# Five moments of issue in a hand-ordered attention and feed-forward kernel on one core

## The chip, the cores and the metric

The kernel runs on one core of one Trainium2 chip. The metric is the device time of one execution in microseconds (us). The engines are called TensorE (PE in the rows; PEld is its loading of weights, which overlaps the matmuls), VectorE (DVE), ScalarE (ACT), GpSimd (POOL) and SyncE (SP), which here only issues DMAs. Each engine works through its own instructions in the order in which the program gives them, and waits on semaphores for the others. Lnnn is a line of the kernel before.

## The reference

Queries, keys and values have 4 batches, 8 heads, 1152 positions and 64 channels. Two neighbouring queries are averaged, so that 576 remain; attention follows. Its output, 4 x 576 x 512, goes through a block that mixes positions and channels by the real part of a two-dimensional Fourier transform, a normalization, and a feed-forward of 512 to 2048 to 512 with two residual sums:

```python
q_pool = q.reshape(B, H, S // 2, 2, D).mean(axis=3)
scores = scale * q_pool @ k.transpose(0, 1, 3, 2)
x = softmax(scores) @ v                      # then (B, 576, 512)
u = x + real(fft(fft(x, axis=1), axis=2))
un = (u - mean(u)) / sqrt(var(u) + 1e-6)
out = u + relu(un @ w_ch1) @ w_ch2
```

The inputs are fp32, with the feed-forward weights handed over as raw 64-bit words that the kernel itself turns into numbers.

## The kernel before

**Attention.** The 32 heads go in 16 pairs, each pair in 5 units (units 0 to 3 take 128 queries of each of the two heads, unit 4 the last 64 of both). For a unit TensorE makes the scores in three pieces of 384 keys (s_piece, L209; two matmuls each, one with the rounded queries qh and one with the rest ql), DVE moves them out with a running bound, ACT takes the exponent in place (s_exp), TensorE transposes the result (t_step, L247), ACT or DVE copies the transposed tiles to SBUF (L250), and TensorE multiplies them with the values (av, L263); ACT copies that into the x buffer of the batch (L267). While unit n is transposed, the scores of unit n+1 are made. The product of a unit (finish, L410) is issued in the next unit, behind its first two score pieces.

**A head's preparation.** In unit 0 and unit 2 of a pair load_head issues the loads of the next pair's two heads: k by POOL's queue, queries, half of k and v by SyncE's queue. There is one buffer qr of raw queries. In units 1 and 3 prep_head (L180) has POOL add neighbouring queries (L186) and make the low part of k (L189); a later event, q_high (L192), has ACT round the queries to qh (L194) and POOL make the rest ql (L197).

**Feed-forward.** Four batches are transformed (dft), normalized (norm) and fed forward (ffn) one after the other. ffn of a batch has 32 blocks in the order q, which, i: four blocks f1 (512 tokens through 128 of the 2048 channels, 12 matmuls, L685 to L687, then ACT's relu L704 and DVE's low part L705) and four blocks f2 (12 matmuls, DVE adds to x at L717). The last four f2 blocks, 28 to 31, end the batch's output and issue its stores (L719). Each block's weights, 512 KB, are read from a scratch in DRAM two blocks ahead into one of three buffers (L677). The last batch also takes the 64 tokens of each batch that the others leave out, works with 384 tokens in two halves, and runs alone at the end.

**Raw weights.** 32 conversions (convert, L614) make that scratch while attention runs: SyncE loads 512 KB of raw words (L617) into one of three buffers, and steps of ACT (L626, L632, L643), DVE (L628, L630, L636, L639) and POOL (L646) follow; SyncE stores the result (L652). From L621 to L649 one conversion is inside at a time; others ask again every 400 units (L619). At most three are under way. A block of the first batch is not issued before the conversion of the block two further on has issued its store (L740). The tiles named wa, rest and wb are taken in turn from four buffers.

**The order.** Nothing is scheduled by a compiler. The program keeps a planner's clock, now, in units of about a nanosecond. attention() yields after each piece of TensorE work and names its cost; each cost gives credit (0.98 or 0.85 of it) to background(), which issues steps of mids (dft and norm, each with a due time) and fills (ffn; 2720 units a block) as long as there is credit. after(wait, fn) puts a step into a heap; it is issued at the first yield whose now is late enough. So a number in after or in a yield decides where in the order of every engine a step stands, and nothing else. When attention is over (tail), fills are issued while mids are not yet due.

**den_recip** (L269) has DVE take the reciprocals of a pair's sums; an event later TensorE transposes them (L276), ACT copies them, SyncE writes them to DRAM and spreads them over 128 rows, and POOL multiplies x by them (DVE in every fourth pair, after which dft of that batch is begun).

**drain** (L793) issues mids and fills, with conversions and events, until block 2h+1 of the last four of a batch has been issued. There are five x buffers (XB); from the sixth on a new one takes the place of one whose output must have been stored, and finish() calls drain just before the first product that is written to it (L411 to L413).

**dft** of the last batch has no gaps between its steps (gap is 0), but two waits of 1200 (L444) and 1800 units (L487): the first behind copies of single rows, the second behind the folds that DVE makes (L450 to L476), ahead of the first transform on TensorE (L497).

Of the kernel before, what the change touches and what calls it, by code (L numbers as in the profile page):

```python
# [12 lines left out]
F32 = mybir.dt.float32  # L13
F32R = mybir.dt.float32r
I32 = mybir.dt.int32
U32 = mybir.dt.uint32
AF = mybir.ActivationFunctionType
# [7 lines left out]
P = 128  # L25
# [18 lines left out]
NP = B * H // 2  # L44
# [10 lines left out]
def fused_kernel(ctx: ExitStack, tc: tile.TileContext, k2, q2, v2, w1, w2, cst, out):  # L55
    nc = tc.nc
# [3 lines left out]
    XB = 5  # L60
# [6 lines left out]
    cvp = pool("cv", 1)  # L67
# [112 lines left out]
    def prep_head(n):  # L180
        kr, qr, ks, vs = raw.pop(n)
        qh, ql = alloc_q(n)
        o = q_cols(n)[0]
        pieces = ((0, SQ, 0),) if o == 512 else ((0, 512, 0), (512, SQ, o))
        for c in (slice(0, HT), slice(HT, SQ)):
            nc.gpsimd.tensor_tensor(qr[:, 0, c], qr[:, 0, c], qr[:, 1, c], op=ALU.add)  # L186
        for i in range(4):
            c = slice(i * HT, i * HT + HT)
            nc.gpsimd.tensor_tensor(ks[D:, c], kr[D:, c], ks[D:, c].bitcast(F32), op=ALU.subtract)  # L189
        qkv[n] = ks, qh, ql, vs  # L190

        def q_high():  # L192
            for a, b, c in pieces:
                nc.scalar.copy(qh[:, c:c + b - a], qr[:, 0, a:b])  # L194
                for x, y in ((a, a + HT), (a + HT, b)) if b - a > HT else ((a, b),):
                    z = slice(c + x - a, c + y - a)
                    nc.gpsimd.tensor_tensor(ql[:, z], qr[:, 0, x:y], qh[:, z].bitcast(F32), op=ALU.subtract)  # L197
        after(2600, q_high)

    sp = {}  # L200
    den = {}
# [54 lines left out]
    def av(pr, j, where):  # L256

        po = ps_o.tile([P, P], F32, tag="o", name="o")
        w = P if j < 4 else D
        for c in range(NKC):  # L260
            for y in range(2):
                pt, o = where[y, c]
                nc.tensor.matmul(po[y * D:y * D + D, :w], lhsT=qkv[2 * pr + y][3][:, c, :], rhs=pt[:, o:o + w],  # L263
                                 start=c == 0, stop=c == NKC - 1)
        if pr not in xt:
            xt[pr] = xt[pr + 1] = xp.tile([P, 2, SQ], F32, tag="x", name="x")
        nc.scalar.copy(xt[pr][:, pr % 2, j * P:j * P + w], po[:, :w])  # L267
# [40 lines left out]
    def attention():  # L308
        first = [load_first(0), load_first(1)]
        for n, (q_load, _, k_load, _, _) in enumerate(first):  # L310
            k_load(*K0[0])
            q_load(*Q0[0])
            for c in K0[1:]:
                k_load(*c)
        nc.sync.dma_start(ident, cst[4, :, :P])
        for q_load, _, _, _, v_load in first:
            q_load(*Q0[1])
        for q_load, _, _, _, v_load in first:
            v_load()
            q_load(*Q0[2])  # L320
        units = [(pr, j) for pr in range(NP) for j in range(5)]
        def parts(n):
            _, q_part, _, k_part, _ = first[n]
            k_part(*K0[0])
            yield q_part(*Q0[0])
            yield k_part(*K0[1])
            yield k_part(*K0[2])

        for _ in parts(0):
            pass  # L330
        for pc, _ in enumerate(parts(1)):
            s_piece(0, 0, pc)
        for _, q_part, _, _, _ in first:
            q_part(*Q0[1])
        s_exp(0, 0)
        for pc in range(3):
            s_piece(1, 0, pc)
        s_exp(1, 0)
        nc.sync.dma_start(onesm, cst[4, :, P:2 * P])
        for _, q_part, _, _, _ in first:  # L340
            q_part(*Q0[2])
        yield 2000
        held = None
        for i, (pr, j) in enumerate(units):
            if pr == 1 and j == 0:
                for x, (t, r) in enumerate(((cc1, P), (cs1, P), (cc2, 97), (cs2, 97))):
                    n, m = t.shape[1:]
                    for r0, r1 in ((0, r // 32 * 32), (r // 32 * 32, r)):
                        if r0 < r1:
                            nc.sync.dma_start(t[r0:r1], cst[x, r0:r1, :n * m].rearrange("p (a b) -> p a b", a=n))  # L350
            if pr + 1 < NP:
                if j in (0, 2):
                    load_head(2 * pr + 2 + j // 2)
                if j in (1, 3):
                    prep_head(2 * pr + 2 + j // 2)
            nxt = unit_tiles(*units[i + 1]) if i + 1 < len(units) else []
            pieces = deque((n, jj, pc) for n, jj in nxt for pc in range(3))
            expd = []

            def some(k):  # L360
                pe = 0
                for _ in range(k):
                    if pieces:
                        p = pieces.popleft()
                        pe += s_piece(*p)
                        if p[2] == 2:
                            expd.append(p[:2])
                return pe

            def exps():  # L370
                while expd:
                    s_exp(*expd.pop(0))

            tiles = unit_tiles(pr, j)
            where = {}

            def tr(items, eng):
                pt = t_step(pr, [(k, c) for k, c, _ in items], eng)
                for x, (_, _, ys) in enumerate(items):
                    for y, o in ys:  # L380
                        where[y, items[x][1]] = pt, x * P + o
                return 105 * len(items)

            if j < 4:
                a, b = tiles
                ga = [[(a, c, [(0, 0)]) for c in cs] for cs in (range(4), range(4, 8))]
                gb = [[(b, c, [(1, 0)]) for c in cs] for cs in (range(4), range(4, 8))]
                gc = [(a, 8, [(0, 0)]), (b, 8, [(1, 0)])]
                g = [ga[0], ga[1], gb[0], gb[1], gc]
            else:  # L390
                k = tiles[0]
                g = [[(k, c, [(0, 0), (1, D)]) for c in cs] for cs in (range(4), range(4, 8), range(8, 9))]
            yield some(2)
            if held:
                yield finish(*held)
            yield tr(g[0], "a")
            yield some(2)
            yield tr(g[1], "a")
            yield some(2)
            for y, x in enumerate(g[2:]):  # L400
                yield tr(x, "v" if j < 4 and y == 1 else "a")
            exps()
            if j == 4:
                after(1500, den_recip(pr))
            held = pr, j, where
            for k in tiles:
                sp.pop(k)
        yield finish(*held)

    def finish(pr, j, where):  # L410
        if j == 0 and pr % 2 == 0 and pr // 2 >= XB:  # L411

            drain(*divmod(pr // 2 - XB, 2))  # L413
        av(pr, j, where)
        if j == 4:
            for y in range(2):
                qkv.pop(2 * pr + y)
        return 1950 if j < 4 else 1000
# [4 lines left out]
    def dft(b):  # L423
# [17 lines left out]
        nc.vector.tensor_copy(ua[D:D + 1, 1, :], tmp[D:D + 1, 0, :])  # L441
        yield 0, gap
        nc.scalar.copy(ub[D:D + 1, 0, :], tmp[D:D + 1, 1, :])
        yield 0, 1200  # L444
        xs = []
        for y, op in ((1, ALU.subtract), (0, ALU.add)):

# [36 lines left out]

        yield from fold(1)
        yield from fold(0)
        yield 0, 1800  # L487

        for y, n in ((1, 256), (0, 257)):

# [121 lines left out]
    going = []  # L612

    def convert(f, which):  # L614
        src = (w1, w2)[which]
        w = cvp.tile([P, 512, 2], I32, tag="wraw", name="wraw", bufs=3)
        nc.sync.dma_start(w, src[f].bitcast(I32).rearrange("p (c x) -> p c x", x=2))  # L617
        yield 4000 if going else 7000
        while inside:  # L619
            yield 400  # L620
        inside.append(f)  # L621
# [6 lines left out]
        nc.vector.tensor_scalar(a, a, WORD_MIN, WORD_MAX, op0=ALU.max, op1=ALU.min)  # L628
        yield 700 if going else 1000
        nc.vector.tensor_scalar(ai, ai, 3, 0x3FFFFFF8, op0=ALU.logical_shift_left, op1=ALU.bitwise_and)  # L630
        rest = cvp.tile([P, 512], F32, tag="cv", name="rest", bufs=4)
        nc.scalar.activation(rest, low.bitcast(U32), AF.Copy, scale=2.0 ** -52)  # L632
        yield 700 if going else 1000
        t = cvp.tile([P, 512], F32, tag="cv", name="wb", bufs=4)
        b = t.bitcast(I32)
# [2 lines left out]
        yield 700 if going else 1000  # L638
        nc.vector.tensor_scalar(ai, b, -0x800000, None, op0=ALU.bitwise_and)  # L639
        yield 700 if going else 1000  # L640
        h = w.rearrange("p c x -> p (c x)").rearrange("p (x c) -> p x c", x=2)
        hi, lo = h[:, 0, :], h[:, 1, :]
        nc.scalar.copy(hi.bitcast(F32R), t)  # L643
# [141 lines left out]
    def after(wait, fn):  # L785

        heapq.heappush(events, (now + wait, next(tick), fn))
# [5 lines left out]
    def drain(b, h):  # L793
        nonlocal now, due, credit
        while (b, 2 * h + 1) not in done_f2:
            if mids and now >= due:
                c = step(mids)
                if c:
                    now += c[0]
                    credit -= c[0]  # L800
                    due = now + c[1]
                continue
            c = step(fills)
            now += c or 300
            credit -= c
            conversions()
            run_events()
# [116 lines left out]
```

## Time and profile before

| | us |
|---|---|
| median of 3 runs | 1041.01 |
| lowest and highest | 1038.89, 1047.71 |
| the profiled execution, its own time | 1044.25 |
| its span, first to last instruction | 1042.5 |
| mean granted share of TensorE's clock | 0.981 |

[...] A row of the waits view is: engine, tile and line that waited, what it waited for, then the sum in us, how often, and the longest. A row of the timeline is: start, duration, engine, line, operation, tiles, shape, count, and in brackets the engine's idle time before it and what ended it.

### The profile page before, as it was taken

Reading aid. Unit: us, or ns where it says so; the run is one execution under the profiler, and the core shown is the slowest. Engines: PE = TensorE matmul, PEld = TensorE weight load, DVE = VectorE, ACT = ScalarE, POOL = GpSimd, SP = SyncE. Lnnn points to the kernel's source line nnn. Section 1 sums busy time; section 2 is a strip of 40 time slices with the busy share of each in tenths; the row PEclk is TensorE's granted clock in tenths of the full one; section 3 lists DMA queues with packets and bytes.
Section 4 is the critical chain, followed back from the end, with each engine's and each line's share of the span. In section 5 each row is a group of like instructions: output and inputs, shape, how many; then the busy total and the mean of one; then the engine's idle time right before and its main releaser. Section 6 shows DMA issues by size and latency. Waiting matters only on the chain.

```text
span 1042.5 us, 19731 instructions
## 1 busy us (share of the span) xinstructions
PE 975.8 (94%) x7392; PEld 847.5 (81%) x7392; DVE 605.4 (58%) x1518; ACT 523.7 (50%) x1017; POOL 421.7 (40%) x609
## 2 busy tenths in 40 slices
PE   6999988898998899899999999999999989999998
PEld 4898977777877777687788888787788867899998
DVE  5556868889754687787644475666544245522222
ACT  5778877767745566466444554554444231201100
POOL 3555678788386575996323141633200010000000
PEclk9999999999999899999999999999999989999999
DMA  6545467646566856475745464163532334733443
GB/s 186 170 135 180 135 197 239 183 127 221 143 203 243 276 181 220 140 240 187 217 145 179 135 193 129 33 207 109 170 104 102 115 120 126 230 134 122 126 136 122
DMA packets 62515, 170.91 MB, mean 164 GB/s; under 512 B 16770, under 2 KB 20242, under 8 KB 62420
## 3 DMA queue, kind: packets, MB, share of 16 engines
q1 hardware_dynamic: 58100, 151.96, 46.1%
q0 software_dynamic: 4320, 17.70, 5.3%
q8 instruction: 58, 0.95, 0.4%
q14 instruction: 37, 0.30, 0.1%
HBM read 146.88 MB, written 22.75 MB: 163 GB/s over the span
## 4 chain that ended last, share of the span: by engine, by line
PE 50%; DVE 5%; POOL 3%; ACT 2%; DMA 2%; issue 1%; SPq 0%; DVEq 0%; ACTq 0%; POOLq 0%
PE f L685 7%; PE f L687 6%; PE f L686 6%; PE s L220 6%; PE o L263 5%; PE t L247 5%; PE t L685 4%; PE t L687 4%; PE t L686 4%; DVE sp L222 1%; DMA out<-x 1%; PE f L505 1%; DMA w<-w 1%; POOL wb L646 1%; POOL rest L646 0%
## 5 line engine op out<-in xcount | busy, mean ns | idle before, releaser
L222 DVE TENSOR_SCALAR_CACHE_REDUCE sp<-s,bia 128x384 f32<-128x384 f32 x288 | 177.2, 615 | 79.2 <-PE s L220 57.2
L220 PE MATMUL s<-ks,qh 128*128 128x384 f32 x480 | 185.7, 387 | 19.8 <-ACT qh L164 6.4
L234 ACT ACTIVATE sp<-sp,bia 128x1152 f32<-128x1152 f32 x144 | 180.2, 1256 | 1.8 <-DVE sp L222 1.6
L263 PE MATMUL o<-pt,vs 128*64 128x128 f32 (+1 forms) x2880 | 171.7, 273 | 9.4 <-DVE pt L250 5.0
L263 PEld LDWEIGHTS o<-pt,vs 128*64 128x64 f32 x2880 | 151.5, 141 | 33.6 <-issue 20.7
L250 ACT COPY pt<-t 128x512 f32<-128x512 f32 (+2 forms) x243 | 124.5, 527 | 91.3 <-PE t L247 90.2
L220 PE MATMUL s<-ks,ql 128*128 128x384 f32 x480 | 164.9, 344 | 0.4 <-POOL ql L165 0.4
L247 PE MATMUL t<-ident,sp 128*128 128x128 f32 x1045 | 150.6, 276 | 7.1 <-DVE sp L222 3.7
L247 PEld LDWEIGHTS t<-ident,sp 128*128 128x128 f32 x1045 | 121.5, 141 | 28.3 <-DVE sp L222 6.7
L220 PEld LDWEIGHTS s<-ks,qh 128*128 128x128 f32 x480 | 92.4, 193 | 31.7 <-ACT pt L250 9.0
L189 POOL TENSOR_TENSOR ks<-kr,ks 64x288 fp32r<-64x288 f32 x120 | 103.4, 894 | 29.7 <-issue 12.6
L705 DVE SCALAR_TENSOR_TENSOR g<-f,g 128x512 fp32r<-128x512 f32 (+1 forms) x52 | 34.7, 667 | 110.0 <-ACT g L704 110.0
L220 PEld LDWEIGHTS s<-ks,ql 128*128 128x128 f32 x480 | 93.1, 194 | 1.1 <-POOL ql L165 0.8
L704 ACT ACTIVATE g<-f 128x512 fp32r<-128x512 f32 (+1 forms) x52 | 30.1, 579 | 119.7 <-PE f L687 119.7
L186 POOL TENSOR_TENSOR qr<-qr 128x288 f32<-128x288 f32 x60 | 49.9, 850 | 92.6 <-DMA qr<-in_q 92.6
L197 POOL TENSOR_TENSOR ql<-qr,qh 128x288 fp32r<-128x288 f32 (+2 forms) x75 | 55.7, 768 | 75.0 <-ACT qh L194 73.7
L685 PE MATMUL f<-unh,w 128*128 128x512 f32 (+1 forms) x208 | 82.8, 398 | 2.7 <-DMA w<-w 2.7
L646 POOL TENSOR_TENSOR rest<-rest,wa 128x256 f32<-128x256 f32 x64 | 48.2, 770 | 89.2 <-DVE wa L639 64.0
L222 DVE TENSOR_SCALAR_CACHE_REDUCE sp<-s 128x384 f32<-128x384 f32 x144 | 78.4, 545 | 6.1 <-PE s L220 4.4
L687 PE MATMUL f<-unl,w 128*128 128x512 f32 (+1 forms) x208 | 80.4, 387 | 0.0
L686 PE MATMUL f<-unh,w 128*128 128x512 f32 (+1 forms) x208 | 80.2, 386 | 0.0
L685 PE MATMUL f<-g,w 128*128 128x512 f32 (+1 forms) x188 | 74.2, 394 | 1.9 <-DVE g L705 0.9
(149 smaller groups left out, 1761.3 us busy)
## 6 DMA issues: line engine op xcount, KB each, us to landing
w<-w SPq DMA_DIRECT2D x128, 512.0 KB
qr<-in_q SPq DMA_DIRECT2D x30, 576.0 KB
ks<-in_k POOLq DMA_DIRECT2D x30, 576.0 KB, 6.1
wraw<-in_w SPq DMA_DIRECT2D x32, 512.0 KB
w<-wraw SPq DMA_DIRECT2D x32, 512.0 KB
vs<-in_v SPq DMA_DIRECT2D x32, 288.0 KB
kr<-in_k SPq DMA_DIRECT2D x30, 288.0 KB
out<-x SPq DMA_DIRECT2D x12, 256.0 KB
```

The costliest lines, as they stand in the source:

```text
L189: nc.gpsimd.tensor_tensor(ks[D:, c], kr[D:, c], ks[D:, c].bitcast(F32), op=ALU.subtract)
L197: nc.gpsimd.tensor_tensor(ql[:, z], qr[:, 0, x:y], qh[:, z].bitcast(F32), op=ALU.subtract)
L220: nc.tensor.matmul(ps, lhsT=l, rhs=k, start=i == 0, stop=i == len(ops) - 1)
L222: nc.vector.tensor_scalar(sp[n, j][:, c], ps, -0.0625, bt[:, pc - 1:pc] if pc else None, op0=ALU.mult, op1=ALU.min, accum_out=bt[:, pc:pc ...
L234: last_exp[0] = nc.scalar.activation(t, t, AF.Exp, bias=bia.pop((n, j))[:, 2:3], scale=-1.0, accum_out=den[pr][:, col:col + 1]).ins
L247: nc.tensor.transpose(ps[:, i * P:i * P + P], sp[k][:, c * P:(c + 1) * P], ident)
L250: (nc.vector.tensor_copy if eng == "v" else nc.scalar.copy)(pt[:, :o], ps[:, :o])
L263: nc.tensor.matmul(po[y * D:y * D + D, :w], lhsT=qkv[2 * pr + y][3][:, c, :], rhs=pt[:, o:o + w], start=c == 0, stop=c == NKC - 1)
L646: nc.gpsimd.tensor_tensor(o[:, c], x[:, c], y[:, c], op=op)
L685: nc.tensor.matmul(ps, lhsT=ah, rhs=bh, start=first, stop=False)
L686: nc.tensor.matmul(ps, lhsT=al, rhs=bh, start=False, stop=False)
L687: nc.tensor.matmul(ps, lhsT=ah, rhs=bl, start=False, stop=last)
```

## The change

Five places are changed, none of which adds or removes an instruction:

- convert: the step behind the load comes 6500 instead of 4000 units later once ffn has begun (going), and the ACT copy rest, with its buffer, is taken three steps later, just ahead of the rounding of the high part;
- prep_head: q_high is issued 5000 instead of 2600 units later;
- den_recip: the transpose is issued 3000 instead of 1500 units later, except in every fourth pair;
- finish: drain for the next pair's x buffer is also called in unit 2 of the pair before;
- dft of the last batch: 1200 becomes 2400, and 1800 becomes 6000.

```diff
@@ prep_head
-        after(2600, q_high)
+        after(5000, q_high)
@@ attention
-                after(1500, den_recip(pr))
+                after(3000 if pr % 4 < 3 else 1500, den_recip(pr))
@@ finish
+        if j == 2 and pr % 2 and (pr + 1) // 2 >= XB and pr + 1 < NP:
+            drain(*divmod((pr + 1) // 2 - XB, 2))
         av(pr, j, where)
@@ dft
-        yield 0, 1200
+        yield 0, 1200 if gap else 2400
...
-        yield 0, 1800
+        yield 0, 1800 if gap else 6000
@@ convert
-        yield 4000 if going else 7000
+        yield 6500 if going else 7000
...
-        rest = cvp.tile([P, 512], F32, tag="cv", name="rest", bufs=4)
-        nc.scalar.activation(rest, low.bitcast(U32), AF.Copy, scale=2.0 ** -52)
         yield 700 if going else 1000
         t = cvp.tile([P, 512], F32, tag="cv", name="wb", bufs=4)
...
         nc.vector.tensor_scalar(ai, b, -0x800000, None, op0=ALU.bitwise_and)
         yield 700 if going else 1000
+        rest = cvp.tile([P, 512], F32, tag="cv", name="rest", bufs=4)
+        nc.scalar.activation(rest, low.bitcast(U32), AF.Copy, scale=2.0 ** -52)
         h = w.rearrange("p c x -> p (c x)").rearrange("p (x c) -> p x c", x=2)
```

## Rows read from the trace of the kernel before

**Rows 1.** Page, part 1: busy us of each engine, share of span, instructions.
```profile
PE 975.8 (94%) x7392; PEld 847.5 (81%) x7392; DVE 605.4 (58%) x1518; ACT 523.7 (50%) x1017; POOL 421.7 (40%) x609
```

**Rows 2.** Windows: PE, PEld, DVE, ACT, POOL busy, clock, DMA share, GB/s.
```profile
125.00:525.00 400.00, 361.22 (x2880) 303.81 (x2876) 292.06 (x697) 251.63 (x487) 279.37 (x386) 0.96 0.62 198
```

**Rows 3.** Waits of the whole span: who <- whom, sum us, times, longest us.
```profile
ACT x L267 <- DMA out<-x: 20.4, 2, 11.4
...
ACT wa L626 <- DMA wraw<-in_w: 16.4, 3, 6.5
ACT qh L194 <- POOL qr L186: 15.3, 7, 3.4
...
ACT rest L632 <- POOL rest L646: 10.6, 4, 4.0
...
DVE wb L636 <- POOL wraw L646: 8.2, 6, 2.2
...
PE t L276 <- DVE den L272: 5.9, 8, 1.5
```

**Rows 4.** Timeline of SP, ACT and PE, 347 to 364: start, us, what, [idle <-releaser].
```profile
347.66 0.34 SPq L652 DMA_DIRECT2D w<-wraw  x1
354.95 0.33 SPq L617 DMA_DIRECT2D wraw<-in_w  x1
...
358.63 0.66 ACT L626 ACTIVATE wa<-wraw 128x512 f32<-128x512 f32 x1 [6.47 <-DMA wraw<-in_w]
...
359.81 4.10 PE L263 MATMUL o<-pt,vs 128*64 128x128 f32 x34 [3.86 <-ACT pt L250]
```

**Rows 5.** Windows behind three of TensorE's waits.
```profile
358.00:365.00 7.00, 5.19 (x37) 4.66 (x38) 3.60 (x7) 5.29 (x10) 4.58 (x7) 0.51 0.89 311
846.00:853.00 7.00, 4.86 (x18) 4.37 (x19) 4.33 (x10) 2.57 (x7) 0.00 (x0) 0.52 0.10 42
299.00:303.00 4.00, 3.48 (x18) 2.98 (x19) 1.93 (x5) 2.54 (x5) 3.92 (x6) 1.00 0.86 317
```

**Rows 6.** Timeline: three waits of PE; POOL and PE at head 9.
```profile
299.52 0.44 PE L220 MATMUL s<-ks,qh 128*128 128x384 f32 x1 [1.72 <-ACT pt L250]
...
432.52 0.44 PE L220 MATMUL s<-ks,qh 128*128 128x384 f32 x1 [2.22 <-DVE sp L222]
442.09 1.19 PE L247 MATMUL t<-ident,sp 128*128 128x128 f32 x6 [2.14 <-DVE sp L222]
...
142.77 1.69 POOL L197 TENSOR_TENSOR ql<-qr,qh 128x288 fp32r<-128x288 f32 x3
144.42 1.43 POOL L646 TENSOR_TENSOR rest<-rest,wa 128x256 f32<-128x256 f32 x2
...
144.57 0.34 PE L220 MATMUL s<-ks,qh 128*128 128x384 f32 x1
```

**Rows 7.** Timeline of PE behind ACT's two waits for output stores.
```profile
507.52 0.93 PE L247 MATMUL t<-ident,sp 128*128 128x128 f32 x6 [2.50 <-ACT pt L250]
...
737.41 0.44 PE L220 MATMUL s<-ks,qh 128*128 128x384 f32 x1 [1.56 <-ACT pt L250]
```

**Rows 8.** Windows: L685 alone (PE, PEld, clock, DMA), and five blocks back to back.
```profile
461.00:499.50 38.50, 11.39 (x28) 5.26 (x28) 1.00 0.62 211
...
824.46:838.18 13.72, 13.72 (x62) 11.34 (x61) 4.12 (x6) 2.00 (x4) 0.00 (x0) 1.00 0.71 207
```

**Rows 9.** Timeline of SP: stores of conversion 29 and of the last, 31.
```profile
472.15 0.32 SPq L652 DMA_DIRECT2D w<-wraw  x1
...
491.95 0.36 SPq L652 DMA_DIRECT2D w<-wraw  x1
```

**Rows 10.** Timeline of PE and DVE in the last transform and normalization.
```profile
848.14 0.74 PE L497 MATMUL t<-cs,xs 128*97 128x128 f32 x2 [4.36 <-DVE xs L473]
...
896.84 0.18 DVE L565 RECIPROCAL vt<-vt 96x6 f32<-96x6 f32 x1
...
901.05 1.43 DVE L597 TENSOR_TENSOR unl<-d,unh 128x576 fp32r<-128x576 f32 x2
```

## Prediction

> **What bounds the kernel now.** I read the page first. TensorE's matmuls are busy for 975.8 us of a span of 1042.5 [rows 1]; no other engine passes 81%, and TensorE's weight loads, which overlap the matmuls, are the one that reaches it. The program is one long TensorE queue, so an edit is worth what it takes out of TensorE's 66.7 us of idle time, plus what the clock gives back. The windows then say where that idle time lies: between 125 and 525 us, where raw weights are converted beside attention, TensorE is busy for 361.22 of 400 us, so 38.8 us of the 66.7 are there, and the mean granted clock is 0.96 [rows 2]. [...] Third, the list of waits: the reader is to look for waits of ScalarE (ACT) and VectorE (DVE) on things that are merely late, since both engines work in order and TensorE waits for them in turn [rows 3]. The rows shown are those that an edit touches. All terms below are made against the profiled execution, 1044.25 us: its span and 1.75 us around it. That is 3.2 above the median of the runs, 1041.01.
>
> **Raw weights (L618, L631).** Nothing is added: 32 conversions keep their instructions. The step that reads the loaded weights is issued 6500 instead of 4000 planner units after the load. What happens now: SyncE may start the load only when the buffer's store has landed, here 354.95 us for a store issued at 347.66; ACT already stands at the step, idle for 6.47 us, until 358.63, and TensorE gets its transposed tile 3.86 us late [rows 4]. There are three such waits, 16.4 us of ACT [rows 3]; only this one shows on TensorE at more than 1 us. 2500 units are some 3 us here, and a conversion that would have jumped the queue with data still in flight now finds an older one ahead of it, so I count 3.9. No weight comes too late for it: conversions run one at a time between L621 and L649 and wait there anyway.
> The copy called rest moves three steps later. It stops ACT 4 times, 10.6 us, for a buffer that GpSimd (POOL) still reads, and DVE 6 times, 8.2 us, in the opposite order of allocation [rows 3]. With the tiles allocated in the new order DVE's step needs the buffer freed by POOL's first pair of operations, and the copy the one freed by its last; but the copy is issued three steps of 700 units later, which are some 3 us here, and POOL's two other pairs take 2 x 1.43 [rows 6]. The TensorE wait at 432.52 us, 2.22 us, stands behind both [rows 6]. Sum 3.9 + 2.2: I take -6, bounds -9 (two smaller waits go too) and +3 (the copy now stands right before the one that POOL waits for).
>
> **Rounded queries (L198).** The ACT copy is issued 5000 instead of 2600 units after POOL's addition that it reads. ACT waited 7 times, 15.3 us, for that addition [rows 3]; TensorE's waits at 299.52 and 442.09, 1.72 and 2.14 us, follow two of them [rows 6], and I count about as much again for the other five: -7.7. Against it: the copy is followed by POOL's subtraction (ql), and POOL is in order. For head 9 ql ended at 142.77 + 1.69 = 144.46 and TensorE read the head at 144.57; directly behind ql stood a conversion, three pairs of POOL operations of 1.43 us, the first at 144.42 [rows 6]. If these are now issued first, ql comes 4.3 us later and TensorE waits about as much. For other heads I add 1.5. SyncE's load of the next head's queries waits for ql also, for up to 2400 units more; that costs only where the next head has no room either, and stands in the upper bound. Together -2; bounds -8 and +10 (three heads caught).
>
> **Transposed reciprocals (L404).** TensorE's transpose waits 8 times for DVE's reciprocal, 5.9 us [rows 3]. In 12 of 16 pairs it is issued 1500 units later, that is behind at least one more unit of TensorE work; the longest wait is 1.5. The other four pairs keep their share. -4, bounds -5 and 0; the scaling behind it is not urgent in these pairs.
>
> **Output stores (L411).** Now the feed-forward of a batch is forced to its output stores at the moment when the next x buffer is wanted. ACT waits for these stores twice, 20.4 us [rows 3]; TensorE then waits 2.50 at 507.52 and 1.56 at 737.41 [rows 7]. Forced three units of attention earlier, the stores have landed: -4. But the forced work is larger. The first time it starts near 460 us, and from 461 to 499.5 TensorE ran 28 of the L685 matmuls, 4 to a block, so 7 blocks must now come in one piece; a block is 13.72 / 5 = 2.74 us [rows 8], together 19.2. Blocks 27 to 29 can be issued only when conversions 29 to 31 have been, of which the stores left at 472.15 and (the last) 491.95 [rows 9]. TensorE runs out of work about 479 us. The conversions then have ACT, DVE and POOL nearly to themselves, and block 29 itself needs only the weights that were stored at 472.15, perhaps 2 us earlier then; a store took up to 7.3 us to land (347.66 to 354.95) and a load 3.7 (354.95 to 358.63) [rows 4]: ready at 482, a wait of 3. The second time, near 690, no conversion is left. So -1 for both; bounds -6 and +10.
>
> **Last transforms (L444, L487).** 1200 to 2400 does nothing: in the planner's count one feed-forward block of 2720 fills either. 1800 to 6000 puts three blocks instead of one ahead of the first transform, and TensorE's 4.36 us of waiting for the folds at 848.14 go [rows 10], since two blocks are 5.5. These two blocks are missing later: in the last normalization, from the reciprocal at 896.84 to the last of the first half at 901.05 + 1.43 us is 5.6 us [rows 10], so far covered by the last two blocks. Some 4 of it come into the open. -1, bounds -7 and +4.
>
> **Clock.** From 358 to 365 us the clock was at 0.51 after the wait of 3.86, and 5.19 us of matmuls cost about 2.6 more; 846 to 853, after 4.36, is alike; 299 to 303, after 1.72, stayed at 1.00 [rows 5]. [...]
>
> **The sum.** -6 - 2 - 4 - 1 - 1 - 6 = -20. Against it stands one allowance. From about 25 us on every event is issued in a new place, and the 38.8 us of idle time are such coincidences; I remove some 14 of them and let half come back elsewhere, +7. So -13: 1031.2 for the execution profiled, 1028.0 against the median.
>
> **Rivals.**
> 1. Everything holds and nothing comes back: -20 or a little more, about 1020. For it: the waits are where the edits are. Against: ACT, DVE and POOL are 63 to 73% busy in that stretch (251.63, 292.06 and 279.37 of 400) [rows 2], so what is late once is easily late again.
> 2. The gain is given back, 1035 to 1045 (about 1039): ql comes behind conversions for two or three heads (+4.3 each), and the clock term stays. For it: head 9's 0.1 us of room. Against: a conversion has to be issued within just these 2400 units, and the last three stores lie 9.9 us apart (472.15 to 491.95, two steps) [rows 9].
> 3. Slower: the first forced stretch. If its three conversions run strictly one behind the other at the pace of now, TensorE has work until 479 and waits for the store of 491.95, 13 us, for its landing and the load, 7.3 and 3.7, and runs at half rate for some us after it, 2. That is +26 against -12 from the rest: +14, 1055. It decides from about 22 us of TensorE waiting in that stretch (-12 + 22 is +1%). Against: block 29 doesn't need the last weights, only their issue.
> 4. The edits don't do what they say, because L618's delay is hidden by the queue at L619: then -7 instead of -13, 1034. I count it with rival 2.
>
> **How the numbers follow.** My forecast, 1024 to 1033, has 0.38; rival 1 has 0.27; rivals 2 and 4 together 0.25; rival 3 has 0.10. 1% is 10.4 us, about what a measurement of this kernel can tell from no change, so faster means below 1030.6: all of rival 1 and two thirds of the forecast, 0.52; slower is rival 3, 0.10; same is the rest, 0.38. The range leaves out 1 in 10 at each end: 1010, 31 below, is three quarters of what all lower bounds together would give (-43, with no allowance), and 1046 lies between rivals 2 and 3.
>
> **What would show it.** Right: no wait of ACT on an output store; TensorE waiting for reciprocals 1 to 2 us in all; the wait at about 848 gone and one of about 4 in the last normalization, near 897; 7 blocks back to back near 460 and again near 690; fewer than 30 us of idle TensorE between 125 and 525. Wrong: ACT still waiting for raw weights, ql ending after TensorE wants the head, or a hole of over 10 us in the first forced stretch.

## The result, and the profile after

The changed kernel takes 1051.53 us, the median of 20 runs (1045.78 to 1057.28); the kernel before, beside it, 1043.74 (1037.74 to 1051.32). The ratio is 1.0075, with a 95% interval of 1.005 to 1.0101: slower by 0.75%, about 8 us, where 1028.0 had been forecast. The profiled execution has a span of 1049.5 us against 1042.5. In the changed kernel every line from L414 on stands two further down, except L633 to L640, which keep their numbers: L685 to L687 are L687 to L689, and L632, the copy that was moved, is L642.

The page, part 1, of the changed kernel, to be held against [rows 1]:

```profile
PE 974.8 (93%) x7392; PEld 847.6 (81%) x7392; DVE 619.3 (59%) x1518; ACT 528.0 (50%) x1017; POOL 420.7 (40%) x609
```

TensorE does the same work and stands idle for 8 us more. The windows of the changed kernel, columns as in [rows 2], and below them the kernel before in the last of these stretches:

```profile
125.00:525.00 400.00, 350.04 (x2800) 293.35 (x2798) 303.74 (x688) 250.65 (x478) 270.83 (x373) 0.94 0.59 190
432.00:443.00 11.00, 4.52 (x13) 2.13 (x14) 9.96 (x14) 0.39 (x1) 4.68 (x7) 0.53 0.34 114
...
466.00:500.00 34.00, 24.51 (x103) 18.92 (x102) 22.51 (x42) 14.63 (x25) 21.36 (x28) 0.90 0.56 196
```

```profile
466.00:500.00 34.00, 32.00 (x232) 26.50 (x232) 25.99 (x60) 20.75 (x38) 24.26 (x34) 1.00 0.66 220
```

Against [rows 2], TensorE is busy for 11.2 us less between 125 and 525, so it stands idle for 50.0 us there, where fewer than 30 would have borne the forecast out, and the mean clock fell from 0.96 to 0.94. Two pieces stand out. From 432 to 443 TensorE is busy for 4.52 of 11 us at half clock; from 466 to 500, the first forced stretch, for 24.51 of 34 instead of 32.00. The waits of the changed kernel, columns as in [rows 3]:

```profile
PE f L507 <- DVE x L517: 11.9, 3, 8.2
...
ACT qh L194 <- POOL qr L186: 8.3, 5, 4.9
...
PE f L580 <- DVE dg L570: 4.8, 1, 4.8
PE s L220 <- POOL ql L197: 4.7, 1, 4.7
```

What was to go has gone: ACT no longer waits for raw weights or output stores, DVE no longer for POOL (8.2 us in [rows 3]), TensorE's 5.9 us of waiting for reciprocals are not in the list, and ACT's wait for the sum of queries is 8.3 instead of 15.3. In their place stand three waits that weren't there. The largest, in the timeline of POOL, DVE and TensorE of the changed kernel:

```profile
424.83 0.59 POOL L126 DMA_DIRECT2D ks<-in_k  x1
425.44 0.81 POOL L512 TENSOR_TENSOR x<-x,bs 128x289 f32<-128x289 f32 x1
...
435.15 1.53 POOL L301 TENSOR_TENSOR x<-x,r 128x288 f32<-128x288 f32 x2
```

```profile
428.05 8.92 DVE L630 TENSOR_SCALAR wa<-wa 128x512 f32<-128x512 f32 x1
436.89 1.53 DVE L517 TENSOR_TENSOR x<-x,f 128x289 f32<-128x289 f32 x4
```

```profile
438.48 1.12 PE L507 MATMUL f<-cc,y 97*1 97x289 f32 x2 [8.21 <-DVE x L517]
```

One DVE instruction, 0.4 to 1.0 us long elsewhere, lasts 8.92 us. It ends at 436.97, when POOL has just come to the end (436.68) of 16 operations without a break. Behind it on DVE stand the additions of the transform, and TensorE waits 8.21 us for them. At 209.85 another lasts 6.39 us in the same way and TensorE waits 3.49 us at 219.11. The other two new waits, on TensorE:

```profile
146.99 0.69 PE L220 MATMUL s<-ks,ql 128*128 128x384 f32 x1 [4.71 <-POOL ql L197]
```

```profile
470.92 0.47 PE L687 MATMUL f<-unh,w 128*128 128x512 f32 x1 [1.54 <-DMA w<-w]
...
484.83 0.64 PE L560 MATMUL f<-onesm,sq 128*96 128x1 f32 x6 [1.44 <-DVE sq L555]
...
490.30 1.33 PE L580 MATMUL f<-dg,onesm 96*128 96x288 f32 x2 [4.82 <-DVE dg L570]
```

The first is head 9, as predicted. The last two are steps of a normalization inside the forced stretch.

### The profile page after: what moved, and what is told of

Read it like the earlier page. It is cut to its first block, busy times and chain, and to the rows that moved or that the text cites. A ratio compares the mean times of both kernels' runs of the same rounds, so it can differ in the third digit from the quotient of the medians.

```text
span 1049.5 us, 19736 instructions
## 1 busy us (share of the span) xinstructions
PE 974.8 (93%) x7392; PEld 847.6 (81%) x7392; DVE 619.3 (59%) x1518; ACT 528.0 (50%) x1017; POOL 420.7 (40%) x609
## 4 chain that ended last, share of the span: by engine, by line
PE 49%; DVE 2%; ACT 1%; issue 0%; DVEq 0%; ACTq 0%
PE s L220 6%; PE f L687 6%; PE f L689 6%; PE f L688 6%; PE o L263 6%; PE t L247 5%; PE t L687 4%; PE t L689 4%; PE t L688 4%; PE f L507 1%; ACT sp L234 0%; ACT pt L250 0%; PE t L507 0%; PE f L499 0%; DVE x L719 0%
## 5 line engine op out<-in xcount | busy, mean ns | idle before, releaser
L263 PE MATMUL o<-pt,vs 128*64 128x128 f32 (+1 forms) x2880 | 169.5, 270 | 7.8 <-DVE pt L250 6.7
L263 PEld LDWEIGHTS o<-pt,vs 128*64 128x64 f32 x2880 | 148.7, 140 | 32.1 <-issue 21.0
L687 PE MATMUL f<-unh,w 128*128 128x512 f32 (+1 forms) x200 | 79.0, 395 | 6.2 <-DMA w<-w 5.8
L687 PE MATMUL f<-g,w 128*128 128x512 f32 (+1 forms) x192 | 75.8, 395 | 1.8 <-DMA w<-w 1.0
L689 PE MATMUL f<-unl,w 128*128 128x512 f32 (+1 forms) x200 | 76.6, 383 | 0.0
L688 PE MATMUL f<-unh,w 128*128 128x512 f32 (+1 forms) x200 | 76.6, 383 | 0.0
```

The source lines that it names most:

```text
L687: nc.tensor.matmul(ps, lhsT=ah, rhs=bh, start=first, stop=False)
L688: nc.tensor.matmul(ps, lhsT=al, rhs=bh, start=False, stop=False)
L689: nc.tensor.matmul(ps, lhsT=ah, rhs=bl, start=False, stop=last)
```

## Experiments

In all of them the time is a ratio to the kernel before, run on the same chip; an interval is 95%. Not all experiments were on one chip, so two of them are compared through their ratios.

### Parts of the change alone

`d_only_drain` makes only this:

```diff
+        if j == 2 and pr % 2 and (pr + 1) // 2 >= XB and pr + 1 < NP:
+            drain(*divmod((pr + 1) // 2 - XB, 2))
```

> Only the earlier call of drain (the output stores' part) is made. Theory A (the first forced stretch, about 466 to 500 us, leaves TensorE without work because norm's own chain of ACT and DVE stands in TensorE's order between the blocks; in the trace of the changed kernel some 9.5 us idle there and 6.8 us at half clock, against two waits of ACT on output stores saved): slower by about 6 us, ratio 1.003 to 1.010, waits of TensorE on norm's lines of 3 to 5 us between 465 and 500, ACT's waits on output stores gone. Theory B (the forced stretch is harmless, the loss comes from the rounded queries): ratio 0.994 to 1.000, with the same waits of ACT gone and under 3 us of new idle time there.

Measured: 1.0016 (0.999 to 1.0042), between the two. ACT's waits on stores are gone; in the forced stretch TensorE waits 3.13 us for weights (470.33) and 3.91 us for norm's dg (485.20). The price is there, but this kernel also gets its gain, TensorE's waits of [rows 7].

`q_only_queries`:

```diff
-        after(2600, q_high)
+        after(5000, q_high)
```

> Only q_high is issued 5000 instead of 2600 units after the addition. Theory A: ql of head 9 stands behind a conversion, one wait of TensorE of 4 to 5 us near 147 us with some 3 us of half clock behind it, against 4 us saved at ACT's waits for the addition: ratio 1.000 to 1.005. Theory B: this edit alone carries the slow-down, ratio 1.006 to 1.012, with the long VectorE instructions (over 5 us for one that takes under 1 us elsewhere) in its trace too.

Measured: 0.9992 (0.9963 to 1.002). TensorE waits 7.0 us for ql, 6.0 of them at 150 us, and ACT's wait for the sum falls from 15.3 to 6.4. No long DVE instruction. Theory B is out.

`r_only_raw` makes both edits of convert, 6500 for 4000 and rest three steps later.

> Only the two edits of the conversions: the longer delay behind the load, and the copy rest three steps later. Theory A: ACT's waits for raw weights go (16.4 us of ACT), and nothing else of note: ratio 0.992 to 0.998. Theory B (the shifted order alone costs as much as such a wait gives): 0.998 to 1.004, with new waits of TensorE of 2 us or more in places that no edit touches.

Measured: 0.9995 (0.9966 to 1.0025). ACT's waits for raw weights are gone, and yet nothing is gained. DVE's timeline of this kernel (L628 is before's number):

```profile
425.51 8.79 DVE L628 TENSOR_SCALAR wa<-wa 128x512 f32<-128x512 f32 x1
```

So the long instruction comes with these two edits, and it comes again in another kernel and execution.

`n_no_drain` is the whole change without the two lines of `d_only_drain`.

> All of the change but the earlier call of drain. Theory A: the wait on ql near 147 us and those behind single long VectorE instructions near 219 and 438 us stay, the forced stretch goes: ratio 1.000 to 1.003. Theory B (the forced stretch is harmless): as the whole change, 1.006 to 1.010. If the long VectorE instructions depend on chance and not on the order, they are absent or elsewhere in this trace and the ratio falls to 0.995 or less.

Measured: 0.9994 (0.9968 to 1.002), with the waits of theory A (4.1 us for ql, instructions of 6.39 and 8.93 us). The early drain therefore costs 0.8% on top of the other edits, though alone it had cost 0.16%. Part of the difference shows in the trace: in `n_no_drain` ACT waits for a store once, 10.3 us, and not twice, and of TensorE's 2.50 and 1.56 us behind the stores [rows 7] only 1.50 (at 508.75) and 0.40 (at 735.01) are left anyway, so the drain has 1.9 us to save instead of 4.1. The other 4 to 5 us of the difference are no larger than its uncertainty and stay unexplained.

`r_delay` is one execution of the longer delay alone, without moving rest.

> Only the longer delay behind the raw weights' load, the copy rest where it was. Theory C: the single long VectorE instructions come with the delay, which moves every conversion against dft's additions: instructions of 3 us or more near 210 and 425 us, TensorE's wait of about 8 us behind the second. Rival: they come with the copy rest, which is now late for POOL; then there is none over 2.1 us here.

It took 1038.61 us. A long instruction is there, but neither expected place nor cause fits: 6.42 us at 252.08, and it is norm's dg (L568), not a conversion. Near 425 there is none. The kernel before has the same instruction, behind the same load of k, at 253.08, 2.04 us long. So it isn't one line of the change that brings it, but where a DVE instruction happens to fall.

### The long DVE instruction

First the adds of dft that make POOL's longest run were given to DVE, which reads the matmul's result in PSUM (first three batches):

```diff
-                    nc.scalar.copy(bs[:, j, :], ps[:, :NH])
+                    if not gap:
+                        nc.scalar.copy(bs[:, j, :], ps[:, :NH])
...
-                        nc.gpsimd.tensor_tensor(u[:, j, :NH], u[:, j, :NH], bs[:, j, :], op=ops[0])
+                        add, src = (nc.vector, ps) if gap else (nc.gpsimd, bs[:, j, :])
+                        add.tensor_tensor(u[:, j, :NH], u[:, j, :NH], src[:, :NH], op=ops[0])
```

and likewise the line below. `f_only` is this on the kernel before:

> None of the change's edits; only dft's additions of bs (L510, L511) in the first three batches move from POOL, where they are a run of eight operations, to DVE, which reads the matmul's result itself, so ACT's copy of it goes. Theory C (a POOL run of this kind holds single VectorE instructions of the conversions for as long as it lasts, but only where such an instruction falls right into it, which the kernel before escapes): in this kernel the move gains nothing, ratio 0.996 to 1.002. Rival (the move is worth something by itself, POOL being 70% busy there, or costs 3 us of DVE per batch): 0.990 to 0.995, or 1.003 to 1.008.

Measured: 0.9996 (0.9966 to 1.0026). `f_no_drain` is this on `n_no_drain`:

> All of the change but the earlier call of drain, with dft's additions of bs on DVE. Theory C: the VectorE instructions of 6.4 and 8.9 us near 209 and 424 us and the waits of TensorE behind them (3.5 and 8.4 us, with 3.4 and 10.2 us of half clock) go, worth 10 us and more: ratio 0.984 to 0.992 against 0.9994 with the additions on POOL. Rival D (each removed coincidence is replaced by others in the re-dealt order): 0.996 to 1.003, with other waits of 2 us and more between 200 and 460 us.

Measured: 0.9905 (0.9874 to 0.9935). What is worth nothing on the kernel before is worth 0.9% on the changed one, some 9 us: the long instructions of 6 and 9 us and the waits behind them are not in this trace (one of 3.8 us is left at 135).

Then POOL's run by itself, `m_port`: DVE's instruction beside 1 to 16 additions of POOL.

> Leaves out all of the computation; it measures one thing. In 60 trials POOL runs 1, 4, 8 or 16 additions of 128x289 and 128x287 fp32 in SBUF (0.7 us each in the trace) without a break, while DVE, after 0.5 to 1 us of additions that read PSUM, does one of three operations of 128x512: tensor_scalar in SBUF, scalar_tensor_tensor of two SBUF tiles, tensor_tensor of SBUF and PSUM. Theory C (POOL's run holds the instruction until it ends): the first two take up to about 0.7 us times the additions still left, 9 to 11 us at 16, at least in some phases, the third takes 0.5 to 0.6 us always. Rival (an instruction gets in behind the addition that is under way): none over 1.5 us, whatever the number.

The rival holds here. Of 40 instructions of the first two kinds the longest takes 1.06 and 1.23 us (the means are 0.65 and 0.90), and no longer beside 16 additions than beside 4; the third kind is always 0.68. POOL's run alone held DVE in none of these trials. But in the traces a DMA that POOL issues itself, the load of k at L126, stands 0.05 to 3.4 us ahead of every instruction over 6 us, with a run of POOL behind it: at 424.83 in the changed kernel, at 252.03 in `r_delay`. `k_moved` takes two of these loads from ahead of dft's run to behind it:

```diff
-        ds = [nc.gpsimd.dma_start(ks, k2[b, h]), nc.sync.dma_start(qr, q2[b, h]),
+        kd = lambda: nc.gpsimd.dma_start(ks, k2[b, h])
+        ds = [after(5000, kd) if n in (13, 20) else kd(), nc.sync.dma_start(qr, q2[b, h]),
```

> As n_no_drain (all of the change but the earlier call of drain), and of POOL's loads of k two, those of heads 13 and 20, are issued behind dft's run of eight additions instead of right ahead of it; the order on TensorE, ACT and DVE is the same as in n_no_drain. Theory E (a VectorE instruction that needs POOL's way to SBUF is held from a DMA issued by POOL until the run of POOL operations behind it ends): the instructions of 6.4 and 8.9 us near 209 and 424 us are under 2 us, TensorE's waits of 3.5 and 8.4 us behind them go, ratio 0.987 to 0.994. Theory C (the run alone holds it): they stay, ratio 0.998 to 1.002.

Measured: 0.9936 (0.9904 to 0.9968). Both instructions are short now, 1.11 and 0.81 us. POOL and DVE in this kernel, at the second place:

```profile
424.15 0.79 POOL L510 TENSOR_TENSOR x<-x,bs 128x289 f32<-128x289 f32 x1
...
429.96 0.59 POOL L125 DMA_DIRECT2D ks<-in_k  x1
...
434.70 1.53 POOL L301 TENSOR_TENSOR x<-x,r 128x288 f32<-128x288 f32 x2
```

```profile
427.35 0.81 DVE L628 TENSOR_SCALAR wa<-wa 128x512 f32<-128x512 f32 x1
...
432.02 4.76 DVE L634 SCALAR_TENSOR_TENSOR wb<-wraw,wa 128x512 int32<-128x512 int32 x1 [0.27 <-POOL rest L646]
```

Beside the same additions L628 takes 0.81 us instead of 8.9. The next instruction of this kind behind the moved DMA is held in its turn, until 436.78; POOL's run behind the DMA ends at 436.23. The transfers in flight beside it did not do it: the loads that SyncE issues right ahead of the short L628, and while it runs, are these, and over its 0.81 us the DMA engines are busy for a share of 0.58.

```profile
426.90 0.34 SPq L617 DMA_DIRECT2D wraw<-in_w  x1
427.33 1.74 SPq L292 DMA_DIRECT2D r<-rd  x3
```

`m_port2` measures it without the kernel:

> Leaves out all of the computation; it measures one thing, as m_port did, with 42 trials: a DMA of 128x1152 fp32 from DRAM, issued by SP, by POOL without a change of type, or by POOL into fp32r as the kernel's load of k, then at once 16 POOL additions of 128x289 and 128x287; DVE comes with its tensor_scalar or its scalar_tensor_tensor of 128x512 after 0 to 6 additions of 128x512 that read PSUM (0.6 us each). Theory E: behind SP's DMA none over 1.5 us; behind POOL's DMA, in some phases, 5 to 12 us, until the run ends. Theory C, already weakened by m_port: no difference between the three.

DVE's timeline of `m_port2`. The first two rows are from the trials with SP's DMA, the next two behind POOL's without a change of type, the fifth behind POOL's into fp32r; the last two are the other operation, with SP's and behind POOL's:

```profile
18.81 0.72 DVE L103 TENSOR_SCALAR a<-a 128x512 f32<-128x512 f32 x1
...
87.00 0.87 DVE L103 TENSOR_SCALAR a<-a 128x512 f32<-128x512 f32 x1
...
109.72 12.48 DVE L103 TENSOR_SCALAR a<-a 128x512 f32<-128x512 f32 x1
...
181.10 8.87 DVE L103 TENSOR_SCALAR a<-a 128x512 f32<-128x512 f32 x1
...
204.23 12.37 DVE L103 TENSOR_SCALAR a<-a 128x512 f32<-128x512 f32 x1
...
299.10 0.98 DVE L105 SCALAR_TENSOR_TENSOR a<-w,a 128x512 int32<-128x512 int32 x1
...
391.74 12.72 DVE L105 SCALAR_TENSOR_TENSOR a<-w,a 128x512 int32<-128x512 int32 x1
```

Behind POOL's DMA all 24 instructions that fall into a run take 8.87 to 12.72 us, and each ends 0.3 to 0.6 us after the last of the 16 additions. In the trials with SP's DMA the twelve take 0.72 to 1.13 us. The instructions that come before their run begins take 0.42 to 0.70. But SP issued its loads in two batches, not each ahead of its own run:

```profile
0.75 7.25 SPq L88 DMA_DIRECT2D kf<-in_k  x7
...
181.21 7.03 SPq L88 DMA_DIRECT2D kf<-in_k  x7
```

They took at most 7.0 us to land, so none was in flight beside these twelve: they show POOL's run without any transfer. For a run beside SyncE's transfers there is the 0.81 us of `k_moved`. `m_port2` has one length of run only; that it is the run's end that counts, and not a fixed time, the kernels show: behind the loads at 209.43 and 424.83 of the changed kernel the run ends 6.3 and 11.9 us after the issue, and the long instruction 6.8 and 12.1 us after it.

Theory E, that an instruction is held from POOL's DMA until the run ends, is shown by these trials, but not without exception. Its words "needs POOL's way to SBUF" were the author's conjecture: no run shows by which way either engine reaches SBUF. In the kernel before, POOL and DVE at the first place:

```profile
207.19 0.59 POOL L126 DMA_DIRECT2D ks<-in_k  x1
...
216.40 1.42 POOL L646 TENSOR_TENSOR wraw<-wb,rest 128x256 fp32r<-128x256 f32 x2
```

```profile
207.28 0.69 DVE L636 SCALAR_TENSOR_TENSOR wb<-wraw,wa 128x512 int32<-128x512 int32 x1 [0.62 <-POOL wraw L646]
...
211.02 0.82 DVE L639 TENSOR_SCALAR wa<-wb 128x512 int32<-128x512 int32 x1
```

L639 falls into the middle of the run and isn't held. `d_only_drain`, `q_only_queries` and `r_delay` have the same, with 0.76, 0.86 and 0.42 us. In all four the instruction before it, L636 here, lay across the start of the run. Whether that lets the next ones through is not shown: at 134.27 in the kernel before, where a shorter run begins beside L636, the next instruction takes 1.80 us.

### The forced stretch

`f_no_q` is `f_no_drain` with 2600 for the queries again:

> As f_no_drain, and the rounded queries at 2600 units as before. Theory A: the wait on ql near 147 us (4.2 us, 3.4 us of half clock) goes, others on the sum of queries come back: 2 to 5 us better than f_no_drain, ratio 0.981 to 0.989. Rival: the queries' edit pays in other places, and f_no_q is 1 to 4 us slower than f_no_drain.

Measured: 0.9919 (0.9891 to 0.9947), the same as `f_no_drain` within the intervals. The wait on ql is gone but for 0.4 us and nothing is gained: neither expectation. `f_late` adds the early drain, but not for pair 9:

```diff
+        if j == 2 and pr % 2 and (pr + 1) // 2 > XB and pr + 1 < NP:
```

> As f_no_q, with the earlier call of drain for the last two buffers that it covers (pairs 11 and 13), not for the first (pair 9). Theory A: only the first forced stretch costs, because conversions and norm's chain are in it; the later one saves ACT's wait on the store near 735 us: 0 to 3 us better than f_no_q. Rival: any forced stretch leaves TensorE idle behind norm's chain, 3 us or more worse than f_no_q.

Measured: 0.9846 (0.9813 to 0.9879), 1027.36 us: faster than both kernels, and 0.7% better than `f_no_q`, more than either theory gave. TensorE's wait of 1.94 us at 726 behind the store is gone. The profiled spans, 1030.4 and 1028.6, lie only 1.8 apart, so the size stays open. `g_first` adds pair 9:

> As f_late (reciprocals, last transforms, both raw-weight edits, dft's additions on DVE, drain early for pairs 11 and 13), with the early call for pair 9 too. Theory A (the first forced stretch alone is what the output stores' edit costs): 5 to 10 us slower than f_late's 0.9846, so ratio 0.989 to 0.995, with waits of TensorE on norm's dg and on weights of 4 us and more in all between 455 and 490 us and half clock behind them. Rival (f_late's gain is mere order, the first call is harmless): within 2 us of f_late.

Measured: 0.9938 (0.9914 to 0.9962): against `f_late` the first forced stretch costs 0.9%, uncertain by 0.4, some 9 us. `g_fills` forces fills alone:

```diff
-            drain(*divmod((pr + 1) // 2 - XB, 2))
+            drain(*divmod((pr + 1) // 2 - XB, 2), pr > 9)
...
-            if mids and now >= due:
+            if both and mids and now >= due:
```

> As g_first, but the forced stretch of pair 9 issues fills alone, no steps of dft and norm. Theory A (norm's chain, uncovered, is what stands in TensorE's way): its waits on sq and dg leave the stretch; 2 to 6 us better than g_first, what stays are waits for weights. Rival, as predicted (TensorE starves behind the conversions): the waits for weights take over, the stretch stays as long as in g_first or grows, and the time is within 1.5 us of g_first or above it.

Measured: 0.9892 (0.9862 to 0.9922). TensorE's longest wait in that stretch of `g_first`, and the windows of `g_first`, then of `g_fills`:

```profile
480.22 1.33 PE L582 MATMUL f<-dg,onesm 96*128 96x288 f32 x2 [4.82 <-DVE dg L572]
```

```profile
455.00:490.00 35.00, 25.76 (x96) 19.34 (x95) 19.76 (x39) 14.14 (x24) 18.89 (x26) 0.80 0.50 173
```

```profile
455.00:490.00 35.00, 32.73 (x254) 27.04 (x252) 20.75 (x47) 17.44 (x31) 20.26 (x28) 1.00 0.64 215
```

With norm's steps left for later the stretch loses its long waits and runs at full clock, and about half of the cost is gone: 0.46% of 0.92%, each uncertain by some 0.4. The waits for weights add up to 1.9 us in both, so the conversions had not been what held TensorE up. What the other half is stays open; no single wait in that stretch of `g_fills` is over 1 us.

## Why the prediction was wrong

- **Raw weights, -6.** The waits went as reckoned and `r_only_raw` is 0.9995. The step that failed is "Nothing is added": the conversions move against POOL's load of k and dft's run, and one DVE instruction is held for 8.8 us. The upper bound, +3, was made from the neighbours that the edit names and had no row for this. The kernel before holds the same parts and escapes: its load at 207.19 has such a run behind it, but none of the DVE instructions there takes over 1.1 us, and near 425 it has no load of k right ahead of the run. "No weight comes too late" isn't borne out either: TensorE's wait for weights between 320 and 328, 2.25 us before, is 4.00 in `r_only_raw` and 3.10 in the changed kernel, though runs without this edit have up to 3.50.
- **Rounded queries, -2.** Measured alone -0.08%, -1 us, uncertain by 3. That it lies near -2 is luck: the two waits counted as gains, 1.72 and 2.14 us, are still there in `q_only_queries`, with 1.74 (at 306.08) and 1.69 (at 450.44). The forecast of head 9 (4.3 us late) holds at 4.71, and at 6.0 in `q_only_queries`.
- **Reciprocals, -4.** The waits went; the time was not measured alone.
- **Output stores, -1.** Here the second step failed. The pieces were right (seven blocks in one go, stores landed, nothing lost near 690), but I looked for idle TensorE only behind the conversions and allowed 3 us. The longest waits were for norm's own chain of DVE and ACT (sq, then dg), for which attention had been the cover: 9.5 us idle between 466 and 500 against 2.0, and with that chain taken out (`g_fills`) about half of the cost goes. As measured, +8 us on the rest of the change. The upper bound of +10 held it; the value taken, nearest to the lower end, did not.
- **Last transforms, -1.** As predicted, the 4.36 us of [rows 10] come back elsewhere, at the place forecast, but 8 us later:

```profile
905.53 1.29 PE L580 MATMUL t<-dg,onesm 96*128 96x288 f32 x4 [1.54 <-DVE dg L570]
...
909.64 0.66 PE L687 MATMUL t<-unh,w 128*128 128x384 f32 x1 [2.82 <-issue]
```

  1.54 + 2.82 = 4.36, so 0 instead of -1 in these waits. The profile names no cause for the second; the time of this edit was not measured alone.
- **Clock, -6.** The sign was wrong, by little: no run shows the 6 us that the sum gives back for the clock (8 of the -43 of all lower bounds). From 125 to 525 the trace has the lower of two levels, 0.50 of the clock against 1.00, for 44.4 us against 30.7 before (the rounded means, 0.94 and 0.96, give 48 and 32). TensorE was busy for only 32.8 of them, against 29.1, and half of that is what the level costs (score matmuls start 0.32 us apart at it, near 149, and 0.17 at the upper, near 355): 16.4 us against 14.5, so 2 us more lost, not 6 given back. 10.2 of the 44.4 lie between 432 and 443, around the one wait, where TensorE had little to do. One trace is one draw: the mean granted clock of the 20 runs of the changed kernel goes from 0.974 (1057.28 us) to 0.984 (1045.78 us).
- **The allowance, +7** for new coincidences, was meant for this kind of loss, and one wait of 8.21 us is more than all of it.

Of the rivals, 3 had the sign, and its place, but not its mechanism. The two causes together make the result: the early drain costs 0.8% on top of the rest, and the long instructions 0.6% (`k_moved`) to 0.9% (`f_no_drain`). Without either the rest of the change gives 0.9905, 1033.5 us, with the additions on DVE, or 0.9936 with two loads moved, both within the stated 1010 to 1046; with them the gain turns into +0.75%.

## What to carry to other kernels

Before moving work in a hand-made order, look on GpSimd for DMAs that it issues itself with a run of its operations right behind: a VectorE instruction that falls there may stand until the run ends, as tensor_scalar and scalar_tensor_tensor on SBUF data did here (8.92 us behind a run of 16 operations and 6.39 behind one of 8 in the changed kernel, 8.87 to 12.72 in `m_port2`), and all that is queued behind it (TensorE for 8.21 and 3.49 us). Issue such a DMA where GpSimd has nothing to do next, or keep the run short; what was measured is two loads moved behind dft's run (`k_moved`: 1.11 and 0.81 us, and a ratio of 0.9936 instead of 0.9994). And when work is forced into one piece, ask of every step in it which other work had covered its chain of engines until now; forcing only the steps that have no such chain removed about half of the cost here (0.46% of 0.92%, `g_fills`).

## What the runs showed of the hardware

A DMA issued by POOL, in fp32 as in fp32r, made DVE's next tensor_scalar or scalar_tensor_tensor of 128x512 last until POOL's run of 16 additions ended: 8.87 to 12.72 us in 24 of 24 trials of `m_port2`, against 0.72 to 1.13 in twelve trials beside the same run with no DMA in flight, and 0.81 in `k_moved` beside loads issued by SyncE. DVE's additions of 128x512 that read PSUM went on beside the run: six took 4.29 us behind POOL's DMA (at 176.90) and 4.29 in the trials with SP's (at 82.79). Four kernels have a place where the instructions behind such a DMA are not held (0.42 to 0.86 us). Why the DMA makes the difference, and what lets these through, no run here shows.
